# First loads over three queues, a first layer by single units, and filler products on TensorE, in a DeltaNet block followed by a gated feed-forward block

## The chip, the cores and the metric

The kernel runs on one core of a Trainium2 chip. The metric is the device time of one execution in microseconds; three runs of a kernel give a median. A profile of one more execution gives the span of that core, which is shorter than the device time of the same run. Engines are PE (TensorE; PEld is its weight load), DVE (VectorE), ACT (ScalarE), POOL (GpSimd) and SP (SyncE, which here only issues transfers).

## The reference

For each of 4 x 8 heads, a state of 48 x 48 is carried through 768 tokens, and the result goes through a feed-forward block:

```python
for t in range(S):
    y[:, :, t] = einsum('bhd,bhde->bhe', q[:, :, t], state)
    v_old = einsum('bhde,bhd->bhe', state, kt)          # kt = k / (|k| + 1e-6)
    state = state + bt * einsum('bhd,bhe->bhde', kt, vt - v_old)
x = y.transpose(0, 2, 1, 3).reshape(3072, 384)
h = x @ w_in                                            # 384 x 2048
out = (h * cos(h)) @ w_out                              # 2048 x 384
```

q, k, v and beta are float32; both weights are float64 in memory, so they arrive as pairs of 32-bit words and are narrowed on the chip.

## The kernel before

The tokens are cut into 24 units of 32 tokens (all heads, all batches); two units make a pair. For each unit, k and q are loaded (`load`, L323; four transfers each), transposed on PE (`turn`, L489), and multiplied with each other (`gram`, L507). The scaled product (`gram_keys`, L518) is written to DRAM (`gram_put`, L538) and read back in another layout (`gram_get`, L547; two transfers per pair). There a triangular inverse is built column by column for a whole pair (`invert`, L576 and L583): for pair 0 on DVE in PSUM, for all the others on POOL. It is written to DRAM (`put`, L592) and read back per unit (`get`, L601; four transfers).

Then comes the serial part: `through_state` (L618) multiplies the unit's keys and queries with the state, `right_side` (L633) subtracts, `solve` (L645) applies the inverse, `solve_out` (L653) scales, `update` (L666) and `update_out` (L674) change the state, `within` (L683) adds the part inside the unit. `features` (L700) transposes the result into `x_ffn`. Unit 0 has no product with the state.

A pair's 256 tokens then pass the feed-forward block: eight steps of `hidden` (L719; six matmuls of 128x128 by 128x256 each, filling one of two PSUM banks `p_h`), each followed by ACT `turns` (L732), DVE `rest` (L736), ACT `cos` (L743, L744) and DVE `gate` (L751), and then the second layer. Pair 0 uses the plain second layer (`output`, L761); later pairs use seven products of Strassen's scheme (`product`, L805, sums on DVE). The weights come in 28 pieces (12 of w_in, 16 of w_out): SP load (L396), ACT split (L404, L406), DVE shift (L410, L415), POOL add (L419). A step of the first layer of pair 0 needs the first 3, 6, 9 or 12 of the w_in adds.

No engine chooses at run time. A planner (`Order`) plays the tasks through when the kernel is built, each with a cost, a due time and the buffers it takes, and writes one order per engine, which the engine then follows strictly. What a task may start with is decided by buffers: `kq`, `one`, `two` and `p_h` in PSUM, nine large SBUF buffers `g` shared by weight pieces, gates and squares. The planner also models the arrival of PE's instructions in blocks of 256 (`stall`), counting the matmuls written so far. Inside the kernel's opening, loads of units 0 and 1, the constants and beta are issued outside the planner, in program order.

```python
load(0, "k")                       # SP
...
load(0, "q", nc.scalar)            # ACT
...
load(1, "q")                       # SP
load(1, "k", nc.gpsimd)            # POOL, behind two transfers of consts and four of beta
```

Of the kernel before, what the change touches and what calls it, by code (L numbers as in the profile page):

```python
# [11 lines left out]
FP = mybir.dt.float32  # L12
I32 = mybir.dt.int32
# [4 lines left out]
C = 32  # L18
DP = 64
SPLIT = 2  # L20
# [26 lines left out]
class Order:  # L47
# [8 lines left out]

    WINDOW = 133.06
    LAG = {"PE": 0.2, "DVE": 0.15, "ACT": 0.15, "POOL": 0.2, "SP": 2.0}
    IN_FLIGHT = 8
    STICK = 4.14  # L60
    CHANGE = 0.15
# [8 lines left out]

    def __init__(self, bufs, free):
        self.bufs, self.free = bufs, free
        self.tasks, self.users, self.tiles = {}, {}, {}
        self.written, self.there = 0, {}

    def add(
# [7 lines left out]
        for tag, t in makes:  # L84
            self.tiles[t] = tag

    def stall(self, key, now, commit):

        n = int(1.007 * self.COUNT[key[0]] + 0.5)
        if key[0] == "state" and key[1] == 0:  # L90
            n = 0
        cost, stall, there = self.tasks[key][1], 0.0, {}
        for i in range(self.written + 1, self.written + n + 1):
            t = now + cost * (i - self.written) / n + stall
            if (i + self.PHASE + self.AHEAD) % self.BLOCK == 0:
                there[(i + self.PHASE + self.AHEAD) // self.BLOCK + 1] = t + self.FETCH
            if (i + self.PHASE) % self.BLOCK == 0:
                block = (i + self.PHASE) // self.BLOCK
                stall += max(0.0, there.get(block, self.there.get(block, 0.0)) - t)
        if commit:  # L100
            self.written += n
            self.there.update(there)
        return stall

    def run(self, wrote):
# [28 lines left out]
        while events:  # L134
# [28 lines left out]
            for engine, heap in ready.items():  # L163
# [3 lines left out]
                item = min(able, default=None)  # L167
                if item is None:
                    continue
                if engine == "PE":  # L170
# [49 lines left out]
def kernel(  # L220
# [58 lines left out]
    def bank(tag, shape, name):  # L279
        bufs = {"kq": 1, "two": 1, "one": 1, "h": 2}[tag]  # L280
        return psum.tile(shape, FP, name=name, tag=tag, bufs=bufs)
# [7 lines left out]
    def quarter(b):  # L289
        return slice(C * b, C * b + C)  # L290
# [43 lines left out]
    near = 130 + C  # L334
    for cols in (slice(0, near), slice(near, consts_np.shape[1])):
        nc.gpsimd.dma_start(out=consts[:, cols], in_=consts_dr.ap()[:, cols])
    ident = consts[:, 0:128]
# [6 lines left out]
    for b in range(B):  # L344
        nc.gpsimd.dma_start(
            out=bq[C * b : C * b + H].rearrange("p n t -> p (n t)"), in_=beta[b]
        )
    load(1, "q")
    load(1, "k", nc.gpsimd)

# [183 lines left out]
    def gram_put(n):  # L534
        m = n // 2
        if m not in gbs:
            gbs[m] = dram.tile([2, H, B, C, C], FP, name="g_dr")
        nc.sync.dma_start(  # L538
            out=gbs[m][n % 2].rearrange("h b j i -> (b j) h i"), in_=gs.pop(n)
        )  # L540

    def gram_get(m):

        g_dr = gbs[m]
        gbs[m] = work.tile([128, C, C], FP, name="gb", bufs=GBS)
        for a in range(SPLIT):
            nc.sync.dma_start(  # L547
                out=gbs[m][half(a)].rearrange("p j i -> p (j i)"),
                in_=g_dr.rearrange("u h b j i -> (u h b) (j i)"),
            )  # L550
# [44 lines left out]

    def get(n):

        zts[n] = work.tile([128, H, C], FP, name="zt")
        z_dr = z_drs[n // 2].rearrange("r s u h b i -> u b (r s) h i")[n % 2]
        for b in range(B):  # L600
            nc.sync.dma_start(out=zts[n][quarter(b)], in_=z_dr[b])  # L601

# [110 lines left out]
    gates, p_hs, turns, rests, p_os, outs = ({} for _ in range(6))  # L713

    def hidden(p, f):
        p_h = p_hs[p, f] = bank("h", [128, 2, TOK], "p_h")
        for i in range(2):
            for t in range(KT):
                nc.tensor.matmul(  # L719
                    p_h[:, i],  # L720
                    w_in[:, t, (f + i) * 128 : (f + i + 1) * 128],
                    xts[p][:, t],
                    start=(t == 0),
                    stop=(t == KT - 1),
                )
# [4 lines left out]
    def hidden_turns(p, f):  # L730
        turns[p, f] = ffn_pool.tile([128, 2, TOK], I32, name="turns")
        nc.scalar.activation(turns[p, f], p_hs[p, f], AF.Copy, scale=TURN)  # L732

    def hidden_rest(p, f):
        r = rests[p, f] = ffn_pool.tile([128, 2, TOK], FP, name="r")
        nc.vector.scalar_tensor_tensor(  # L736
            out=r, in0=p_hs[p, f], scalar=TURN, in1=turns.pop((p, f)),
            op0=ALU.mult, op1=ALU.subtract,
        )
# [6 lines left out]
    def hidden_gate(p, f):  # L746
        if f % 4 == 0:
            gates[p, f // 4] = ffn_pool.tile(
                [128, 4, TOK], FP, name="g_ffn", tag="g", bufs=GATES
            )  # L750
        nc.vector.tensor_tensor(  # L751
            out=gates[p, f // 4][:, f % 4 : f % 4 + 2],
            in0=rests.pop((p, f)),
            in1=p_hs.pop((p, f)),
            op=ALU.mult,
        )
# [105 lines left out]
    def store(p, i):  # L862
# [4 lines left out]
        )  # L867


    order = Order(  # L870
# [4 lines left out]
        ),  # L875
        free={"SP": 5.5, "ACT": 5.6, "POOL": 6.2, "DVE": 6.0, "PE": 6.0},
    )
    add = order.add
    VECTOR = {0: "one"}
    W_IN, W_OUT, LOADS = 62.2, 48.42, -16.83  # L880
    PLAIN = range(1)
    outs_done = [None]
    START = 64.59
    FIRST, STEP = 4.18, 5.64
    BASE = [START + (8 * FIRST + (p - 1) * 8 * STEP if p else 0) for p in range(NU // 2 + 2)]

    def inverse(m):
        add(("gram_get", m), "SP", 1.2, lambda: gram_get(m),
            [("gram_put", 2 * m), ("gram_put", 2 * m + 1)], makes=[("gb", ("gb", m))],
            uses=[("g_dr", m)], moves=2.2)  # L890
        held = VECTOR.get(m)
        z = ("p_i", m) if held else ("z", m)
        add(("eye", m), "ACT", 0.65, lambda: invert_eye(m, held),
            [("gram_put", 2 * m + 1)] + ([("eye", m - 1)] if m else []),
            makes=[(held or "z", z)])
        deps = [("eye", m), ("gram_get", m)]
        ends = [0, 4, 8, 12, 16, 20, 24, C - 1]
        for i, (x, y) in enumerate(zip(ends, ends[1:])):
            each = (0.2, 0.001) if held else (0.323, 0.00178)
            cost = sum(  # L900
                2 * (each[0] + each[1] * (j // SPLIT + 1) * (C - 1 - j)) for j in range(x, y)
            )
            add(("inv", m, i), "DVE" if held else "POOL", cost,
                lambda x=x, y=y: invert(m, held, range(x, y)), deps,
                uses=[("gb", m)] if y == C - 1 else [])
            deps = [("inv", m, i)]
        if held:
            add(("inv_out", m), "ACT", 0.65, lambda: invert_out(m), deps,
                makes=[("z", ("z", m))], uses=[z])
            deps = [("inv_out", m)]  # L910
        add(("put", m), "SP", 0.45, lambda: put(m), deps, makes=[("z_dr", ("z_dr", m))],
            uses=[("z", m)], moves=2.6)

    def unit(n):
        m, second = n // 2, n % 2
        for x, prev in (("k", 2 * len(kps)), ("q", 2 * len(qps)), ("v", 4)):
            if n < 2 and x != "v":
                add((x, n), "SP", 0.0, lambda: None)
                continue
# [50 lines left out]
        if second:  # L970
            inverse(m)
        add(("get", n), "SP", 1.9, lambda: get(n), [("put", m)], makes=[("zt", ("zt", n))],
            uses=[("z_dr", m)], moves=1.4)

# [5 lines left out]
            uses=[("vp", m)] if n else [])  # L980
        add(("solve", n), "PE", 0.75, lambda: solve(n), [("right", n), ("get", n)],
            makes=[("one", ("p_u", n))], uses=[("zt", n), ("rhs", n) if n else ("vp", m)])
# [18 lines left out]
    def gated(p):  # L1001
        for f in range(0, FT, 2):
            deps = [("features_out", 2 * p + 1)]
            if p == 0:
                deps += [("add", t) for t in range(KT * (f // 4 + 1))]
            if p or f:
# [10 lines left out]
            add(("gate", *key), "DVE", 0.73, lambda f=f: hidden_gate(p, f),  # L1017
                [("cos", *key)] + ([("gate", p, f - 2)] if f % 4 else []),
                makes=[] if f % 4 else [("g", ("gates", p, f // 4))],
                uses=[("h", *key), ("r", *key)], due=BASE[p] + f // 2 * STEP + 8)  # L1020
# [11 lines left out]
    def plain(p):  # L1032
        last = outs_done[0]
        for i in range(2):
            for k in range(FT // 4):
                deps = [("gate", p, 4 * k), ("gate", p, 4 * k + 2)]
                if p == 0:
                    deps += [("add", 12 + t) for t in range(4 * k + 4)]
                if last:
# [74 lines left out]

    add(("beta",), "DVE", 1.3, spread_beta)
    for n in range(NU):
# [69 lines left out]
```

## Time and profile before

| | |
|---|---|
| device time, median of 3 runs | 712.05 us (711.9 to 712.48) |
| the profiled run | 709.21 us, span 707.4 us, mean granted clock 0.955 |
| PE busy | 642.0 us, 91% of the span |
| DVE, ACT, POOL busy | 400.3, 281.5, 344.1 us |
| chain that ended last | PE 85%, DMA 4%, POOL 3%, DVE 3%, issue 2% |
| first matmul of the first layer (L719) | 79.15 us |

The profile cuts the span into 40 slices of 17.7 us and gives the busy share of each engine in tenths. PEclk is the granted clock of PE in tenths of the full one. In the chain, "issue" is time in which an engine waited for nothing that the profile shows. An arrow with an engine or a transfer names what ended an idle time.

### The profile page before, as it was taken

Reading aid. Unit: us, or ns where it says so; the run is one execution under the profiler, and the core shown is the slowest. Engines: PE = TensorE matmul, PEld = TensorE weight load, DVE = VectorE, ACT = ScalarE, POOL = GpSimd, SP = SyncE. Lnnn points to the kernel's source line nnn. Section 1 sums busy time; section 2 is a strip of 40 time slices with the busy share of each in tenths; the row PEclk is TensorE's granted clock in tenths of the full one; section 3 lists DMA queues with packets and bytes.
Section 4 is the critical chain, followed back from the end, with each engine's and each line's share of the span. In section 5 each row is a group of like instructions: output and inputs, shape, how many; then the busy total and the mean of one; then the engine's idle time right before and its main releaser. Section 6 shows DMA issues by size and latency. Waiting matters only on the chain.

```text
span 707.4 us, 25090 instructions
## 1 busy us (share of the span) xinstructions
PE 642.0 (91%) x11000; PEld 564.3 (80%) x11000; DVE 400.3 (57%) x804; ACT 281.5 (40%) x482; POOL 344.1 (49%) x738
## 2 busy tenths in 40 slices
PE   3206989999999999999999999999999999999985
PEld 2205767768988988988988988988989989988975
DVE  4995568967655645546546546545635535544441
ACT  4423467742443532532533533533433433432420
POOL 6468957868608508518518518518318328200000
PEclk9555899999999999999999999999999999999999
DMA  9888663562223233133223133231221220100000
GB/s 176 211 161 197 122 193 80 135 125 58 36 56 71 39 64 67 32 74 66 45 60 66 29 77 64 38 74 37 38 51 37 37 52 14 31 23 4 1 23 22
DMA packets 162700, 49.25 MB, mean 70 GB/s; under 512 B 154208, under 2 KB 157296, under 8 KB 162592
## 3 DMA queue, kind: packets, MB, share of 16 engines
q1 hardware_dynamic: 161120, 46.82, 32.1%
q8 instruction: 86, 1.41, 0.9%
q0 software_dynamic: 384, 0.64, 0.4%
q10 hardware_dynamic: 1088, 0.20, 0.2%
q14 instruction: 22, 0.18, 0.1%
HBM read 36.62 MB, written 11.01 MB: 67 GB/s over the span
## 4 chain that ended last, share of the span: by engine, by line
PE 85%; DMA 4%; POOL 3%; DVE 3%; issue 2%; ACT 1%; SPq 1%; ACTq 0%; DVEq 0%; POOLq 0%
PE p_h L719 35%; PE p_out L805 30%; PE p_kq L618 4%; PE p_kq L683 3%; PE p_s L666 3%; PE p_out L761 3%; PE p_u L645 3%; PE p_t L489 2%; PE p_g L507 2%; DMA pairs<-in_moe_w_in_dram 2%; POOL part L576 1%; POOL z L583 1%; DMA qp<-in_q_dram 1%; DMA gb<-g_dr 1%; DMA kp<-in_k_dram 1%
## 5 line engine op out<-in xcount | busy, mean ns | idle before, releaser
L719 PE MATMUL p_h<-x_ffn,w_in 128*128 128x256 f32 x1152 | 264.9, 383 | 2.4 <-DVE g_ffn L751 1.6
L719 PEld LDWEIGHTS p_h<-x_ffn,w_in 128*128 128x128 f32 x1152 | 216.9, 191 | 32.0 <-DVE g_ffn L751 1.5
L576 POOL TENSOR_TENSOR part<-z,gb 128x126 f32<-128x126 f32 (+22 forms) x341 | 136.1, 399 | 210.7 <-DMA gb<-g_dr 185.3
L583 POOL TENSOR_TENSOR z<-z,part 128x126 f32<-128x126 f32 (+22 forms) x341 | 134.3, 394 | 26.7
L805 PE MATMUL p_out<-w_out,g_ffn 128*128 128x192 f32 x704 | 133.6, 334 | 2.8 <-DVE o L853 1.6
L736 DVE SCALAR_TENSOR_TENSOR r<-p_h,turns 128x512 f32<-128x512 f32 x96 | 66.1, 689 | 113.8 <-ACT turns L732 113.7
L732 ACT ACTIVATE turns<-p_h 128x512 int32<-128x512 f32 x96 | 56.9, 592 | 169.1 <-PE p_h L719 169.0
L805 PEld LDWEIGHTS p_out<-w_out,g_ffn 128*128 128x128 f32 x704 | 113.6, 190 | 9.5 <-ACT o L842 3.3
L805 PE MATMUL p_out<-w_sum,g_ffn 128*128 128x192 f32 x528 | 96.3, 329 | 1.8 <-DVE o L853 1.8
L751 DVE TENSOR_TENSOR g_ffn<-r,p_h 128x512 f32<-128x512 f32 x96 | 65.6, 683 | 48.0 <-ACT r L744 48.0
L805 PEld LDWEIGHTS p_out<-w_sum,g_ffn 128*128 128x128 f32 x528 | 86.3, 190 | 4.9 <-DVE o L853 3.1
L821 DVE TENSOR_TENSOR g_ffn<-g_ffn 128x256 f32<-128x256 f32 x176 | 80.5, 480 | 10.8 <-PE p_out L805 8.9
L743 ACT ACTIVATE r<-r 128x512 f32<-128x512 f32 x96 | 60.7, 632 | 58.2 <-DVE r L736 58.1
L744 ACT ACTIVATE r<-r,halfpi 128x512 f32<-128x512 f32 x96 | 69.3, 722 | 3.1
L853 DVE SCALAR_TENSOR_TENSOR o<-p_out,o 128x192 f32<-128x192 f32 x77 | 26.5, 356 | 59.7 <-PE p_out L805 59.2
L489 PE MATMUL p_t<-consts,kp 128*128 128x128 f32 x96 | 16.9, 306 | 41.9 <-DMA vp<-in_v_dram 29.5
L489 PEld LDWEIGHTS p_t<-consts,kp 128*128 128x128 f32 x96 | 12.9, 157 | 44.6 <-issue 38.5
L694 ACT COPY y<-p_kq 128x384 f32<-128x384 f32 x24 | 11.5, 478 | 76.7 <-PE p_kq L683 76.7
L448 POOL TENSOR_TENSOR knrm<-ksum,halves 128x16 f32<-128x16 f32 (+1 forms) x14 | 36.4, 2602 | 9.8 <-DVE ksum L436 7.6
L618 PEld LDWEIGHTS p_kq<-st,kq_t 48*32 48x32 f32 x2944 | 29.5, 106 | 9.6 <-issue 8.8
L618 PE MATMUL p_kq<-st,kq_t 48*32 48x48 f32 x2944 | 33.1, 215 | 3.9 <-issue 3.2
L653 DVE TENSOR_TENSOR u<-p_u,bz 128x768 f32<-128x768 f32 x24 | 23.0, 956 | 17.1 <-PE p_u L645 17.1
(65 smaller groups left out, 547.0 us busy)
## 6 DMA issues: line engine op xcount, KB each, us to landing
pairs<-in_moe_w_in_dram SPq DMA_DIRECT2D x12, 512.0 KB
gb<-g_dr SPq DMA_DIRECT2D x24, 256.0 KB
pairs<-in_moe_w_out_dram SPq DMA_DIRECT2D x16, 384.0 KB
vp<-in_v_dram SPq DMA_DIRECT2D x96, 48.0 KB
out_dram<-o SPq DMA_DIRECT2D x24, 192.0 KB
kp<-in_k_dram SPq DMA_DIRECT2D x92, 48.0 KB
qp<-in_q_dram SPq DMA_DIRECT2D x92, 48.0 KB
g_dr<-g SPq DMA_DIRECT2D x24, 128.0 KB
```

What stands on the lines that cost most here:

```text
L489: nc.tensor.transpose(p_t[:, a, j], src[:, 2 * j : 2 * j + 2], ident)
L576: eng.tensor_tensor(out=part, in0=z[:, 0:rows, j, None].to_broadcast(shape), in1=a[:, j, None, j + 1 :].to_broadcast(shape), op=ALU.mult,)
L583: eng.tensor_tensor(out=behind, in0=behind, in1=part, op=ALU.subtract)
L618: nc.tensor.matmul(p_kq[quarter(b), par, a, j], kq_t[rows48(par), a, j, quarter(b)], st[rows48(par), b // 2, j, b % 2], start=(j == 0 and ...
L719: nc.tensor.matmul(p_h[:, i], w_in[:, t, (f + i) * 128 : (f + i + 1) * 128], xts[p][:, t], start=(t == 0), stop=(t == KT - 1),)
L732: nc.scalar.activation(turns[p, f], p_hs[p, f], AF.Copy, scale=TURN)
L736: nc.vector.scalar_tensor_tensor(out=r, in0=p_hs[p, f], scalar=TURN, in1=turns.pop((p, f)), op0=ALU.mult, op1=ALU.subtract,)
L743: nc.scalar.activation(r, r, AF.Abs)
L744: nc.scalar.activation(r, r, AF.Sin, bias=halfpi, scale=-2.0 * math.pi)
L751: nc.vector.tensor_tensor(out=gates[p, f // 4][:, f % 4 : f % 4 + 2], in0=rests.pop((p, f)), in1=p_hs.pop((p, f)), op=ALU.mult,)
L805: nc.tensor.matmul(p_o, left(p, e // 2, a)[:, e % 2], right(e, b), start=(e == 0), stop=(e == FT // 2 - 1), skip_group_check=True,)
L821: nc.vector.tensor_tensor(out=left(p, k, to), in0=left(p, k, one), in1=left(p, k, two), op=op)
```

## The change

Three things are done, and the planner's constants are set anew, so that the order changes on all engines.

1. Loads. k of unit 1 moves from POOL to SP, ahead of q of unit 1; the far part of the constants moves on POOL behind beta. Pair 0's second `gram_get` transfer, and two of the four `get` transfers of units 0 and 1, move from SP to ACT's queue.
2. First layer of pair 0 by single units (`hidden_one`): a step takes four column tiles for one unit's 128 tokens, twelve matmuls of 128x128 by 128x128, in place of two column tiles for 256 tokens. Steps 0 to 3 need unit 0 alone, and the gates of all four groups are opened by them.
3. Filler (`warm_up`): where the planner sees PE idle between 44 and 80 us of its own clock, it writes a product of the identity with constants, 128x128 by 128x256, into the PSUM bank of the second layer, which nobody reads. 37 of them are written: 21 after the gram of units 2 and 3; 4 after the turn of unit 4; 4 and 2 around the update of unit 0; 3 and 3 around that of unit 1.

```diff
-    WINDOW = 133.06
+    WINDOW = 74.02
+    WARM = 44.0, 80.0
-    STICK = 4.14
+    STICK = 4.01
@@ stall
-        n = int(1.007 * self.COUNT[key[0]] + 0.5)
+        n = int(n * 1.034 if self.written < 1000 else n * 1.0054 + self.rest)
@@ run
                 if item is None:
+                    if engine == "PE" and self.WARM[0] <= now < self.WARM[1]:
+                        self.warm()
+                        self.written += 4
+                        free[engine] = now + 0.45
...
@@ opening
-    for cols in (slice(0, near), slice(near, consts_np.shape[1])):
-        nc.gpsimd.dma_start(out=consts[:, cols], in_=consts_dr.ap()[:, cols])
+    nc.gpsimd.dma_start(out=consts[:, :near], in_=consts_dr.ap()[:, :near])
...
+    nc.gpsimd.dma_start(out=consts[:, near:], in_=consts_dr.ap()[:, near:])
+    load(1, "k")
     load(1, "q")
-    load(1, "k", nc.gpsimd)
@@
+    def hidden_one(f):
+        unit, k = f // 8, f // 2 % 4
+        p_h = p_hs[0, f] = bank("h", [128, 4, 128], "p_h")
+        for i in range(4):
+            for t in range(KT):
+                nc.tensor.matmul(p_h[:, i],
+                    w_in[:, t, (4 * k + i) * 128 : (4 * k + i + 1) * 128],
+                    xts[0][:, t, unit * 128 : (unit + 1) * 128],
+                    start=(t == 0), stop=(t == KT - 1))
+    def warm_up():
+        nc.tensor.matmul(flat_out[:, 0:256], ident, consts[:, 0:256], start=True, stop=True)
@@
-    W_IN, W_OUT, LOADS = 62.2, 48.42, -16.83
+    W_IN, W_OUT, LOADS = 57.87, 67.5, 4.07
-    START = 64.59
-    FIRST, STEP = 4.18, 5.64
+    START = 40.69
+    FIRST, STEP = 3.12, 5.86
@@ inverse, pair 0
+            add(("gram_get", m), "SP", ..., lambda: gram_get(m, range(1)), puts, ...)
+            add(("gram_get2", m), "ACT", ..., lambda: gram_get(m, range(1, 2), nc.scalar), puts, ...)
@@ unit, n < 2
+            add(("get", n), "SP", ..., lambda: get(n, range(2)), [("put", m)], ...)
+            add(("get2", n), "ACT", ..., lambda: get(n, range(2, 4), nc.scalar), [("put", m)], ...)
@@ gated, p == 0
+                deps = [("features_out", f // 8)]
+                deps += [("add", t) for t in range(KT * (f // 2 % 4 + 1))]
@@ plain, p == 0
+                    deps = [("gate", p, 8 * i + 2 * k)]
```

In the new order, POOL computes the norms of pair 2 (L448) behind the inverse of pair 1 rather than inside it, and then all eight open w_in adds in a row. SP issues the last three w_in pieces one after another, ahead of k of unit 6.

## The prediction

> **What bounds the kernel now.** I read the page first, its slices before its sums. PE is busy 91% of the span, but the first slices are not, and the granted clock is low exactly there:
>
> ```profile
> PE   3206989999999999999999999999999999999985
> PEclk9555899999999999999999999999999999999999
> DMA  9888663562223233133223133231221220100000
> ```
>
> From the sixth slice on PE is the bound: in the stretches of 10 us from 160 to 680 it stands at 9.3 to 10.0. Nothing in that stage is removed or added, so only the first 110 us can change the time. Next, the stretches of that stage (columns: length, then busy us and instructions of PE, PEld, DVE, ACT, POOL, granted clock, DMA share, GB/s):
>
> ```profile
> 50.00:60.00 10.00, 3.95 (x72) 3.32 (x72) 6.26 (x10) 3.39 (x6) 8.76 (x16) 0.50 0.73 162
> 60.00:70.00 10.00, 8.02 (x355) 7.01 (x355) 5.45 (x13) 3.99 (x8) 9.00 (x15) 0.50 0.93 205
> 70.00:80.00 10.00, 8.09 (x258) 6.94 (x241) 6.31 (x10) 4.19 (x8) 8.58 (x14) 0.63 0.68 119
> 80.00:90.00 10.00, 9.67 (x165) 8.01 (x164) 4.85 (x10) 6.08 (x12) 9.25 (x7) 1.00 0.67 152
> 90.00:100.00 10.00, 8.12 (x239) 6.73 (x238) 8.72 (x18) 8.39 (x17) 5.33 (x12) 1.00 0.90 271
> 100.00:110.00 10.00, 8.90 (x126) 7.14 (x130) 4.41 (x8) 3.01 (x7) 4.91 (x10) 0.83 0.15 41
> ```
>
> Units 0 and 1 are solved at half clock, transfers run at 0.7 to 0.9 of their time, POOL is full. Third, PE in order of time (start, length, instruction):
>
> ```profile
> 53.45 1.09 PE L489 MATMUL p_t<-consts,kp 128*128 128x128 f32 x4 [29.49 <-DMA vp<-in_v_dram]
> 57.04 2.01 PE L645 MATMUL p_u<-vp,zt 32*32 32x48 f32 x64 [1.65 <-issue]
> 79.15 5.45 PE L719 MATMUL p_h<-x_ffn,w_in 128*128 128x256 f32 x24
> 88.48 0.88 PE L645 MATMUL p_u<-rhs,zt 32*32 32x48 f32 x64
> 101.10 0.30 PE L618 MATMUL p_kq<-st,kq_t 48*32 48x48 f32 x10 [2.99 <-issue]
> 101.33 4.53 PE L719 MATMUL p_h<-x_ffn,w_in 128*128 128x256 f32 x12
> ```
>
> A solve costs 2.01 us at 57 and 0.88 at 88. A stall of 2.99 us without a named cause splits the state product of unit 3; after it a first-layer step takes 4.53 us in place of 2.8, as the clock has dropped. (The wait at 53.45 carries a false name: vp isn't read there. The turn of unit 4 needs the bank that DVE's `tt` of unit 3 leaves at 53.35.) Last, POOL and SP:
>
> ```profile
> 38.86 0.24 POOL L576 TENSOR_TENSOR part<-z,gb 128x31 f32<-128x31 f32 x1 [10.39 <-DMA gb<-g_dr]
> 64.67 2.90 POOL L448 TENSOR_TENSOR knrm<-ksum,halves 128x16 f32<-128x16 f32 x1
> 73.61 2.53 POOL L419 TENSOR_TENSOR w_in<-w_in,pairs 128x512 uint32<-128x512 uint32 x2
> 73.96 0.40 SPq L592 DMA_DIRECT2D z_dr<-z  x1
> 78.69 5.86 SPq L601 DMA_DIRECT2D zt<-z_dr  x8
> ```
>
> POOL's inverse of pair 1 runs from 38.86 to 73.66. Behind it stand eight w_in adds (1.26 us each) and, over two transfers, the solve of unit 2 at 88.48. So the ramp has two chains: PE's own (53 to 79) and POOL's.
>
> **What the Trainium skill says.** "TensorE: Matmul & The Clock Gate", Part 1 (What's actually happening): after an idle window of some 3.4 us the clock is half, after a busy one full. The trace agrees: 0.50 through the pauses up to 76, full after PE ran without a pause from 72.71 on; about 4 us. Same page, LDWEIGHTS: a load costs columns / 1.2 ns, an estimate of 107 ns for 128 columns, so a 128-wide pass can still hide it. Turns, which load for every 128-wide pass, start 0.44 us per four (116.63 to 117.07), 110 ns each: agreed. "DMA: Bandwidth & Descriptors", Issuing engines are not separate DMA queues: a second issuing engine saves only issue time. Here an issue takes about 0.45 us (L323: 1.79 for four) against 4 to 6 us to landing.
>
> **The change part by part.** *Loads.* k of unit 1 lands at 12.07 today, 5.04 us after its last issue. SP's queue would have it earlier, perhaps by 2 us. But SP then issues four more transfers (1.8 us) before the `gram_put`s it reaches at 16.75, and the bytes ahead are the same at some 200 GB/s. The ACT half of `gram_get` stands behind ACT's split of the third weight piece (20.52 to 21.7 today), and the eye copy, the fourth split and DVE's fourth shift, which precedes the inverse, queue behind ACT's wait. I let DVE's inverse start at 27.6 as now (bounds −1.5, +1.5) and POOL's at 38.9 (same bounds). The ACT half of `get` saves two issues, 0.9 us, of the 57.04; ACT's next split waits behind it, with slack.
>
> *Filler.* Nothing holds the 21: they run right behind the gram that ends at 24, over by 42 even at half clock (0.86 us each; at full clock 0.43, as L719's 2.59 us for six of this size), and PE idles again until 53.4. They cost and give nothing. The turn (2.0 us) and four fillers (3.45 at half clock) make 5.5 us without a pause up to 58.9, more than the 4 us seen; so full clock before 59. The solve of unit 0 waits for them: 58.0 instead of 56.5, but takes 0.88, ending at 58.9 against 59.05. Then, at full-clock durations from this trace: fillers 1.73 (DVE's u, 0.96, hides inside), update 0.89, within 0.88, fillers 0.86, features 0.5, state 1.3: 65.2. New step 0 of the first layer 2.6: 67.8. Solve 0.88, fillers 1.3, update, within 1.77, fillers 1.3, features 0.5, state 1.3, gram 0.86: 75.8. Today's PE starts its first step at 79.15 and does that gram only at 84.53.
>
> *POOL.* Norms out of the inverse: it ends at 70.7 (73.66 − 2.9); norms then, adds 4 and 5 by 76.2: step 1 can't start sooner. That step and the turn of unit 5 end at 79.8. For unit 2, `put` at 70.8, then eight k and q transfers (3.6 us), `get` 75 to 77, landing after 2.4 to 4 us: 79.5 to 81. I take the solve of unit 2 at 81.5 (bounds 79 and 85).
>
> *Comparing there.* Today's PE has, at its 88.48, one first-layer step (2.6) and one gram (0.86) more behind it. Lead: 88.48 − 81.5 − 3.46 = **3.5 us** (bounds 0 and 6).
>
> *Stalls.* Today's loses 2.99 + (4.46 − 2.79) = 4.66 us at 98 to 106. Counting two weight loads and two passes per matmul (one each for a transpose), this stall and the smaller one at 71.97 (0.74) lie 1,274 apart, five blocks of 256 less a few; the new counts fit both to within two. So the planner now knows the places. But its wait of 3.5 us for a block is short: the block asked for 38 instructions before the last boundary came after some 7.5 us in both stalls, with transfers dense. In the new order four boundaries after 81 (second step there, state of unit 3, solve of unit 3, state of unit 4) leave 3 to 4.6 us. I keep 1.5 us of loss: **−3.2** (bounds −4.7 and +3). Two before 81 (state products of units 1 and 2) are in the 4 us that separate PE's 75.8 from 79.8 and in the bound of 85.
>
> *N = 128.* 8 steps x 24 passes x 3 ns: **+0.6** (bound: 0 and +3, if loads show). Gates write 512 elements as before: 0. ACT and DVE work per step is unchanged.
>
> Sum: −3.5 − 3.2 + 0.6 = −6.1 against the span of 707.4. That run took 709.21 while the three others have a median of 712.05; I take the same difference off: **706.0 us**.
>
> **The rivals.** A, everything early: transfers land 1.5 us sooner, no stall: lead 6, stall −4.7, the pause of 1.28 at 136.5 gone too: −12, 700. For it: exact block counts. Against: DMA at 0.9.
> B, the clean start is eaten: fillers mostly run too early, the solve of unit 2 comes at 84, stalls like today's at the new places: −1.0 + 0.6 and up to 1 either way: 711.5, no change. For it: the 7.5 us.
> C, slower: the fillers are paid at half clock. One place: PE between 55 and 77. If the clock isn't released before the first layer's step 0 (4.3 us, part slow), then solve, fillers, update, within, fillers, features, state take 2.0 + 3.45 + 3.06 + 1.7 + 0.9 + 1.8 = 12.9 from 58.9: step 0 ends at 76, and the 7.9 us of full-clock work, step 1 and turn bring the solve of unit 2 to 88: lead −3; with N = 128 and stalls as today 715.5. It decides as soon as that solve starts later than 85. Against it: 4 us without pause sufficed twice, at 12 to 17 and 72 to 76.
> D, the change doesn't do what it says: the clock stays as today and no step of unit 0 comes early, only the norms' shift acts: 2.9 us earlier for POOL less some handing over, −2, 710.
>
> **How the numbers follow.** Main case 45%, 706; A 20%; B 18%; C 12%; D 5%. The range from 698.5 to 713 holds main, A, D and most of B and leaves C out. A measurement tells some 0.2% (1.4 us) from no change. Faster: main, A, D and a third of B: 0.76. Same: the rest of B: 0.12. Slower: C: 0.12.
>
> **What would show it.** Granted clock 1.0 from about 58 and solve of unit 0 at 0.9 us; 21 fillers over long before 53; first layer from 65; POOL's inverse of pair 1 ended near 70.7; solve of unit 2 near 81.5; "issue" waits of PE after 81 under 2 us. Wrong if the inverse of pair 0 starts more than 2 us off 27.6, if fillers run at half clock at 60, or if a step of twelve takes over 2.8 us.

## The result, and the profile after

The changed kernel is slower: 720.84 us (719.69 to 723.42) against 711.97 us (711.5 to 712.48), four runs each; ratio 1.0129, interval 1.0098 to 1.0161. The profiled run took 719.78 us with a span of 717.8 us, 10.4 us over the span of before (8.9 us by the medians).

The slices of the page, in the same three rows as before:

```profile
PE   4807889989999999999999999999999999999995
PEclk9967799999999999999999999999999999999999
DMA  7886474364214134134135035043122120100000
```

From the tenth slice on PE is as full as before. The clock row is less low (6 and 7 tenths in place of 5), but low up to the same 90 us. The stretches of 10 us (columns as before):

```profile
50.00:60.00 10.00, 4.04 (x14) 3.62 (x15) 6.81 (x11) 1.92 (x4) 8.83 (x16) 0.50 0.72 170
60.00:70.00 10.00, 7.68 (x249) 5.93 (x248) 4.24 (x6) 5.34 (x11) 8.43 (x21) 0.99 0.76 223
70.00:80.00 10.00, 9.09 (x172) 8.25 (x175) 3.29 (x6) 1.35 (x4) 9.53 (x13) 0.66 0.47 79
80.00:90.00 10.00, 7.76 (x302) 6.98 (x292) 8.21 (x14) 3.03 (x6) 6.55 (x5) 0.88 0.25 59
100.00:110.00 10.00, 7.72 (x139) 7.12 (x138) 7.52 (x15) 5.69 (x13) 6.00 (x9) 0.90 1.00 205
```

The clock is full at 60, as intended, and gone again at 70. PE in order of time (start, length, idle before it and what ended that) shows why:

```profile
55.96 1.09 PE L504 MATMUL p_t<-consts,kp 128*128 128x128 f32 x4 [21.52 <-DMA vp<-in_v_dram]
57.69 3.17 PE L914 MATMUL p_out<-consts 128*128 128x256 f32 x8
60.79 0.88 PE L664 MATMUL p_u<-vp,zt 32*32 32x48 f32 x64
70.91 0.96 PE L637 MATMUL p_kq<-st,kq_t 48*32 48x48 f32 x58 [2.27 <-issue]
71.80 5.49 PE L740 MATMUL p_h<-x_ffn,w_in 128*128 128x128 f32 x24
86.60 0.23 PE L637 MATMUL p_kq<-st,kq_t 48*32 48x48 f32 x1 [2.24 <-issue]
87.40 4.57 PE L740 MATMUL p_h<-x_ffn,w_in 128*128 128x128 f32 x24
92.77 0.88 PE L664 MATMUL p_u<-rhs,zt 32*32 32x48 f32 x64
107.66 0.37 PE L702 MATMUL p_kq<-u,tt 32*32 32x48 f32 x14 [2.23 <-issue]
107.95 4.57 PE L740 MATMUL p_h<-x_ffn,w_in 128*128 128x128 f32 x24
129.71 0.31 PE L637 MATMUL p_kq<-st,kq_t 48*32 48x48 f32 x14 [1.50 <-issue]
156.46 5.71 PE L757 MATMUL p_h<-x_ffn,w_in 128*128 128x256 f32 x19 [2.89 <-DVE g_ffn L794]
```

Four waits without a named cause cut small products in two, each at one of the counted block ends (every 256 instructions), and three of them are followed by a step of the first layer at 4.57 to 5.49 us in place of 2.9. The solve of unit 2 starts at 92.77, later than before (88.48). The last line is something new: PE stands 2.89 us for a gate of the second pair. How much was lost ahead of it, the first step of pair 1 tells, where both kernels have done the same products, the fillers apart. Before, and changed:

```profile
118.91 2.86 PE L719 MATMUL p_h<-x_ffn,w_in 128*128 128x256 f32 x12
```

```profile
129.96 5.45 PE L757 MATMUL p_h<-x_ffn,w_in 128*128 128x256 f32 x24
```

The changed kernel is 11.05 us behind there, 14.9 us at 311.20 (326.11), and 10.66 us where the last products of the second layer begin (674.96 and 685.62): a loss as large as the final one is made in the first 130 us. POOL and SP, on the other hand, kept to the forecast within some 2 us: the inverse of pair 1 runs from 41.00 to 72.0, and

```profile
72.11 0.39 SPq L610 DMA_DIRECT2D z_dr<-z  x1
77.34 1.88 SPq L620 DMA_DIRECT2D zt<-z_dr  x4
```

so `zt` of unit 2 was issued 13 us ahead of the solve that needs it. PE's own chain set the time, not POOL's.

### The profile page after: what moved, and what is told of

The parts are those of the page before. It is cut to its first block, busy times and chain, and to the rows that moved or that the text cites. A ratio compares the mean times of both kernels' runs of the same rounds, so it can differ in the third digit from the quotient of the medians.

```text
span 717.8 us, 25428 instructions
## 1 busy us (share of the span) xinstructions
PE 659.3 (92%) x11170; PEld 584.2 (81%) x11170; DVE 400.7 (56%) x804; ACT 281.2 (39%) x482; POOL 340.6 (47%) x734
## 4 chain that ended last, share of the span: by engine, by line
PE 87%; DMA 4%; DVE 4%; issue 2%; SPq 1%; ACT 1%; POOL 0%; ACTq 0%; DVEq 0%
PE p_h L757 32%; PE p_out L848 29%; PE p_kq L637 4%; PE p_h L740 4%; PE p_kq L702 3%; PE p_u L664 3%; PE p_s L685 3%; PE p_out L804 3%; PE p_t L504 2%; PE p_g L522 2%; PE p_out L914 1%; DVE p_i L601 1%; DVE part_v L594 1%; PE p_z L719 1%; SPq L338 1%
## 5 line engine op out<-in xcount | busy, mean ns | idle before, releaser
L757 PE MATMUL p_h<-x_ffn,w_in 128*128 128x256 f32 x1056 | 243.9, 383 | 4.7 <-DVE g_ffn L794 2.9
L594 POOL TENSOR_TENSOR part<-z,gb 128x126 f32<-128x126 f32 (+22 forms) x341 | 131.6, 386 | 219.6 <-DMA gb<-g_dr 194.0
L757 PEld LDWEIGHTS p_h<-x_ffn,w_in 128*128 128x128 f32 x1056 | 198.0, 191 | 31.9 <-issue 5.5
L601 POOL TENSOR_TENSOR z<-z,part 128x126 f32<-128x126 f32 (+22 forms) x341 | 137.7, 404 | 26.7
L848 PE MATMUL p_out<-w_out,g_ffn 128*128 128x192 f32 x704 | 130.6, 332 | 2.4 <-DVE o L896 1.6
L848 PE MATMUL p_out<-w_sum,g_ffn 128*128 128x192 f32 x528 | 93.9, 327 | 1.6 <-DVE o L896 1.6
L740 PE MATMUL p_h<-x_ffn,w_in 128*128 128x128 f32 x192 | 29.3, 321 | 0.6 <-issue 0.6
```

The lines of the kernel that those rows point to most:

```text
L594: eng.tensor_tensor(out=part, in0=z[:, 0:rows, j, None].to_broadcast(shape), in1=a[:, j, None, j + 1 :].to_broadcast(shape), op=ALU.mult,)
L601: eng.tensor_tensor(out=behind, in0=behind, in1=part, op=ALU.subtract)
L740: nc.tensor.matmul(p_h[:, i], w_in[:, t, (4 * k + i) * 128 : (4 * k + i + 1) * 128], xts[0][:, t, unit * 128 : (unit + 1) * 128], start=(t ...
L757: nc.tensor.matmul(p_h[:, i], w_in[:, t, (f + i) * 128 : (f + i + 1) * 128], xts[p][:, t], start=(t == 0), stop=(t == KT - 1),)
L848: nc.tensor.matmul(p_o, left(p, e // 2, a)[:, e % 2], right(e, b), start=(e == 0), stop=(e == FT // 2 - 1), skip_group_check=True,)
```

## The experiments

All ratios are to the kernel before, whose median was 710.1 to 712.1 us. "Anew" means that the planner made its orders again.

**Each part on the kernel before.** First the loads alone (x4), an edit that leaves the order of all computation:

```diff
+    nc.gpsimd.dma_start(out=consts[:, near:], in_=consts_dr.ap()[:, near:])
+    load(1, "k")
     load(1, "q")
-    load(1, "k", nc.gpsimd)
...
+            (nc.scalar if m == 0 and a else nc.sync).dma_start(
...
+            (nc.scalar if n < 2 and b > 1 else nc.sync).dma_start(out=zts[n]
```

> The kernel before with the first loads dealt out as in the change, alone: k of unit 1 on SP, far consts behind beta, half of the first inverse's input and of its first two results on ACT. PE's order is that of before. Theory L: the inverse of pair 0 starts 2 to 2.5 us later than 27.6 and the time rises by 1.5 to 3 us. Theories S and F: within 1 us of before.

Measured 0.9987 (0.9972 to 1.0002). The inverse of pair 0 starts at 29.59, 2 us later than before, but the first step of the first layer at 78.33 (before 79.15): the delay is absorbed. The other way round, the changed kernel with its loads as before (x2):

> The changed kernel with all first loads as before: k of unit 1 on POOL behind consts and beta, second half of the inverse's input and of its result on SP. Order of everything else the same. Theory L: the inverse of pair 0 starts at 27.6 to 28 instead of 30.1, that of pair 1 at 39 instead of 41.0, and the time falls by 2 to 3 us. Theories S and F: the ramp starts earlier but PE stalls at the same instructions (14th record of the within of unit 0, 70th of the state of unit 1 and so on), and the time falls by under 1.5 us.

Measured 1.0079 (1.0052 to 1.0105), but the span is 716.6, 1.2 us under the changed kernel's; the waits sit at the same instructions (2.57, 2.35 and 2.70 us), and DVE's inverse still starts at 30.16. By the medians up to 0.5% could be the loads' (the intervals touch), by the spans 1.2 us; on the kernel before they cost nothing. They are not the main cause. Then the counts alone (x7), and the planner's numbers alone (x10):

```diff
-        n = int(1.007 * self.COUNT[key[0]] + 0.5)
+        n = int(n * 1.034 if self.written < 1000 else n * 1.0054 + self.rest)
```

> The kernel before with the changed kernel's count of instructions alone in the planner (1.034 up to 1000, 1.0054 and the rest carried on after), the plan made anew; loads, layer, constants as before. The prediction's step (the better counts put small products clear of the block ends and save 3.2 us after the solve of unit 2): 703 to 706 of span, ratio 0.990 to 0.997, no wait of 2 to 3 us in the state product of unit 3. Theory (the counts move the waits, since a block takes 4 to 9 us to come in the first 130 us and any order runs into some end): ratio 0.998 to 1.004, with a sum of waits for instructions before 130 us that is within 2 us of that of before.

Measured 1.0011 (0.9997 to 1.0026). A wait of 3.11 us at 102.80 stands where before had 2.99 at 101.10: knowing the counts did not take it away.

```diff
-    WINDOW = 133.06
+    WINDOW = 74.02
...
-    W_IN, W_OUT, LOADS = 62.2, 48.42, -16.83
+    W_IN, W_OUT, LOADS = 57.87, 67.5, 4.07
-    START = 64.59
+    START = 40.69
```

> The kernel before with the changed kernel's numbers of the planner alone (window, STICK, due times), its loads, pairs of units and counts as before, the plan made anew. Theory N (the numbers cost by themselves): slower, ratio 1.003 to 1.012, with a wait of PE of 2 us or more for a gate of the second pair near 150. Theory S (the numbers do nothing but set other places for block ends): 0.997 to 1.005 and no such wait.

Measured 1.0091 (1.0071 to 1.0111). PE waits 5.55 us for gates up to 200 us. But the reverse, the changed kernel with the old numbers (x9),

> The changed kernel with the planner's numbers (window, STICK, due times of w_in, w_out and of the first layer) as before; loads, single units, counts and fillers as changed, the plan made anew. Theory N (the new numbers make w_out's pieces due later than the second pair's gates need DVE for, so PE waits 2.9 to 4.6 us for a gate of the second pair near 150, and the order of the first 100 us is worse): ratio 0.997 to 1.008, no wait of over 1.5 us for a gate between 130 and 170. Theory S (only the place of the block ends and the fillers' time count): ratio 1.008 to 1.02 again, waits for instructions of 6 us or more in sum before 130 us.

came to 1.0142 (1.0088 to 1.0196), with a wait of 2.71 us for instructions at 126.20 and 3.32 us for gates. Its start is better: four steps, all at full clock and with no wait for a gate, are done at the solve of unit 2 (92.45), where the changed kernel has done two (92.77). At the same products it is 9.1 us ahead of the changed kernel at 194 us, and 2.6 us at the end: most of it is lost again in the steady part. The numbers are no cause that could be undone by itself: each set has its own plan, and a plan is good or bad with all the rest.

**Fillers and block ends.** The changed kernel with its plan kept and `warm_up` emitting nothing (x1):

```diff
-        nc.tensor.matmul(flat_out[:, 0:256], ident, consts[:, 0:256], start=True, stop=True)
+        pass
```

> The changed kernel without the 37 fillers, all else in the same order on every engine. Theory S (instruction supply: PE runs through blocks of 256 instructions in 1.3 to 5 us where their arrival took 3.5 to 9 us from the end of the block before, and each stall also halves the clock): the block ends move by up to 148 instructions to other places, the clock stays at half through the solves of units 0 and 1, so fewer stalls there (under 2 us together before the solve of unit 2, against 5.5), and the time falls by 1 to 4 us. Theory F (the fillers themselves hold the chain up: they run 1 to 3 us past what they hide): time falls by 4 to 8 us, solve of unit 2 at 87 or earlier. Theory L (the dealt-out loads start the inverse of pair 0 late): no change, within 1 us, and the inverse of pair 0 still starts near 30.1.

Measured 1.0170 (1.0123 to 1.0217), slower still. The solve of unit 2 comes at 88.45, 4.3 us earlier, and the first step of pair 1 8 us earlier (121.86 against 129.96), only 2.95 us behind the kernel before at the same products. All of that gain is lost later: without the 37 fillers the block ends lie 148 instructions elsewhere, and between 200 and 700 us PE waits 8.0 us for instructions (changed kernel: 1.9; waits over 0.3 us summed). The three largest waits come at 258.45, 418.93 and 579.0, every 160 us: the plan repeats, so one bad place is paid again and again. Against the kernel before this version is 1.1 us behind at 142 us and 15.8 us where the last second-layer products begin, each time at the same products. Now the 21 early fillers alone left out (x3),

```diff
+        warms[0] += 1
+        if warms[0] > 21:
+            nc.tensor.matmul(flat_out[:, 0:256], ident, consts[:, 0:256], start=True, stop=True)
```

> The changed kernel without the 21 fillers that run at 24 to 34 us, long before the solve; the other 16 stay. Nothing waits for those 21, so by theories F and L nothing changes (within 1 us). Theory S: the block ends move by 84 instructions, so the stalls leave their places: none inside the within of unit 0 at its 14th record; instead at or behind its end (42 records later), in the state of unit 1 near record 112 instead of 70, and the stall of 2.2 us in the within of unit 2 moves to the state of unit 3 (near its 4th record). Total within 3 us either way.

which lie in an idle place that ends 20 us after them: 1.0250 (1.0199 to 1.0302). The waits of the solve moved by 84 instructions, the number that was left out, and 8.0 us of waits came up between 200 and 700 us. And all 37 early, none in the solve (x5; all places from the solve of unit 2 on as in the changed kernel):

> The changed kernel with all 37 filler products in the idle place behind the gram of unit 3 and none in the solve; the number of instructions ahead of the solve of unit 2, and so every later place of a block end, is as in the changed kernel. Theory (the later sixteen fillers cost their 9.4 us in a serial chain, and what the kernel without fillers then lost was the moved block ends): the solve of unit 2 starts at 88 to 89.5 as without fillers, the waits after it stay where the changed kernel has them (about 2.2 us in the within product of unit 2, 1.5 in the state product of unit 4) and the steady part shows no waits of 2 us for instructions; span 710 to 714, ratio to before 0.998 to 1.008. Rival (the fillers keep the clock up and pay for themselves): more steps at half clock between 60 and 100, ratio 1.012 or more. Rival (the solve's start doesn't matter, a later wait takes the gain): solve of unit 2 at 88.5 but span 716 to 719.

Measured 1.0147 (1.0092 to 1.0201). The theory falls: the sixteen later fillers (9.4 us of PE) are gone from the solve, and its unit 2 still starts at 92.83:

```profile
69.43 1.11 PE L637 MATMUL p_kq<-st,kq_t 48*32 48x48 f32 x70 [0.69 <-issue]
81.17 1.76 PE L637 MATMUL p_kq<-st,kq_t 48*32 48x48 f32 x126 [1.18 <-DVE st L693]
85.97 0.28 PE L637 MATMUL p_kq<-st,kq_t 48*32 48x48 f32 x1 [3.04 <-issue]
87.12 4.91 PE L740 MATMUL p_h<-x_ffn,w_in 128*128 128x128 f32 x24
```

PE comes to the same block end earlier and waits longer there: it goes on at 85.97, the changed kernel at 86.60. Products at half clock and waits for DVE took the rest. This version and the one without fillers differ only by 37 fillers in an idle place, done 15 us before PE's next product: the 148 instructions of shift alone move the first step of pair 1 from 121.86 to 129.96. Last, the kernel before with 57 fillers in its idle place, which move its block ends by 228 (x8):

```diff
+                if key == ("gram", 3):
+                    self.warm()
...
+        for _ in range(57):
+            nc.tensor.matmul(flat_out[:, 0:256], ident, consts[:, 0:256], start=True, stop=True)
```

> The kernel before, its order untouched, with 57 filler products in the idle place behind the gram of unit 3: they move the later instructions by 228 against the block ends, so that the ends lie 28 instructions further on in the order. Theory (waits are set by the place of the block ends alone): the solve of unit 2 within 1 us of 88.5, the waits of 2.99 and 1.67 us in the state product of unit 3 and behind it gone or moved by 28 instructions, others of the steady part moved too; span 702 to 710, ratio 0.994 to 1.004. Rival (idle-time products cost or give nothing, the waits belong to the data): waits of 2.99 and 1.67 at the same instructions, ratio 0.998 to 1.002. Rival (fillers warm the clock): first solve shorter by 1 us or more and the lead kept to the end.

Measured 0.9989 (0.9963 to 1.0016). The wait of 2.99 us moved by those 28 instructions, to 106.52 (1.88 us), and in place of one of 0.74 us at 72.71 stand two of 0.97 and 1.27 us at 67.90 and 72.76: the waits follow the places, and their sum from 60 to 200 us is no smaller, 4.1 us against 3.7.

**w_out's pieces.** One number back, anew (x12):

```diff
-    W_IN, W_OUT, LOADS = 57.87, 67.5, 4.07
+    W_IN, W_OUT, LOADS = 57.87, 48.42, 4.07
```

> The changed kernel with one number back, the due time of w_out's pieces (48.42 in place of 67.5), the plan made anew. Theory N in its narrow form (w_out's pieces come too late, and DVE does them together with the second pair's gates at 142 to 157): the wait of 2.89 us for a gate at 156 gone, ratio 1.003 to 1.010. If w_out isn't it: the wait stays within 1 us, ratio 1.010 or more. If the pieces of w_in are pushed back by it, the first step of the first layer comes after 73 and the solve of unit 2 after 94.

Measured 1.0084 (1.0055 to 1.0113). The wait at 156.46 is gone, the longest for a gate of the second pair is 1.20 us, and the solve of unit 4 still comes at 165.83; the waits for instructions stay (2.27, 2.12 and 3.18 us). The solve of unit 2 stands at 92.83 as in the changed kernel, but with one first-layer step and one gram more behind it, some 3.7 us of work. This is a part of the loss, not the loss.

**Pairs again, with and without fillers.** The first layer by pairs, loads, fillers, numbers and counts as changed, anew (x6):

```diff
-        if p == 0:
-            return hidden_one(f)
...
```

> The changed kernel with the first pair's first layer by pairs of units again (tiles of 256 columns), loads, fillers, counts and the planner's constants as changed; the plan is made anew. Theory (single units cost nothing in themselves, the fillers and the waits for instructions do): still 1.004 to 1.016 over before, the first hidden step of the first pair not before 84, fillers of 9 us or more still in the chain, steps at half clock still there. Rival (the single units are the loss: twice the instructions and twice the weight loads): within 0.3% of before, the solve of unit 2 at 87 to 89.

Measured 1.0206 (1.0157 to 1.0255): the slowest version but one. Without fillers in it and in the planner's count (x11):

```diff
-                        self.written += 4
...
-        nc.tensor.matmul(flat_out[:, 0:256], ident, consts[:, 0:256], start=True, stop=True)
+        pass
```

> The kernel before with the new loads, counts and numbers of the planner, but without single units and without fillers, the plan made anew. If the fillers made the version by pairs the slowest of all (1.0206): ratio back at 0.998 to 1.006, the solve of unit 2 at 87 to 89. If the numbers did (theory N): ratio 1.010 to 1.02 still, with the wait for a gate near 150.

Measured 1.0006 (0.9986 to 1.0026). PE's order up to 126 us is the same in both but for the fillers and one swap of neighbours, and up to the solve of unit 2 the version *with* fillers is ahead (90.73 against 92.56). Then SP's orders part. Without fillers, the four pieces of w_out in one go:

```profile
128.18 4.64 SPq L410 DMA_DIRECT2D pairs<-in_moe_w_out_dram  x4
149.66 5.57 PE L754 MATMUL p_h<-x_ffn,w_in 128*128 128x256 f32 x24 [1.00 <-DVE g_ffn L788]
```

With fillers, three of the four stand behind q and v on SP's queue, POOL waits 5.10 us, DVE's shifts pile up in front of a gate, and PE waits 4.65 us for it:

```profile
135.28 2.91 SPq L411 DMA_DIRECT2D pairs<-in_moe_w_out_dram  x3
136.82 1.02 POOL L434 TENSOR_TENSOR w_out<-w_out,pairs 128x384 uint32<-128x384 uint32 x1 [5.10 <-DMA vp<-in_v_dram]
154.03 7.55 PE L755 MATMUL p_h<-x_ffn,w_in 128*128 128x256 f32 x24 [4.65 <-DVE g_ffn L789]
```

A further 6.8 us of waits for instructions fall between 200 and 700 us there, against 0.9 without fillers. So fillers might cost by themselves, or only through the plan and the places. A square of four tells it: pairs or single units, with no fillers or with 64 that the planner doesn't count. 64 fillers are 256 instructions, one whole block, so the later block ends stay where they are, and all orders are kept (18 is 26 for the single units, which have fewer idle places).

```diff
+        warms[0] += 1
+        for _ in range(18 if warms[0] == 1 else 1):
+            nc.tensor.matmul(flat_out[:, 0:256], ident, consts[:, 0:256], start=True, stop=True)
```

> The version by pairs without fillers (x11), every order of every engine kept, plus 64 fillers that the planner doesn't count: 46 in the idle place behind the gram of unit 3, 18 in the places of the solve where the plan has PE idle. 64 fillers are 256 instructions, so every later block end stays where it was. Theory P (fillers themselves save 1 to 2 us, by the clock, and what cost 2 per cent in x6 was the plan that they moved: w_out's pieces behind k, q and v on SP's queue): the solve of unit 2 at 90.5 to 92, no wait of over 1.5 us for a gate near 150, ratio 0.995 to 1.001. Rival F (fillers cost in themselves, wherever): ratio 1.008 or more, the wait near 150 back.

> The changed kernel without fillers and without their count in the plan, made anew: the new loads, counts, numbers, and single units in the first layer. Beside x11 it differs in the single units alone. If single units cost by themselves (twice the instructions for the same columns, so more block ends in the dense part): 1.004 to 1.012 over before. If they are neutral: 0.998 to 1.004, as x11. A wait for a gate near 150 of over 2 us would say that the plan, not the units, is what is seen.

> x14 with 64 fillers that the planner doesn't count (46 early, 18 in the solve), all orders and all later block ends as in x14. Theory P: against x14 by 0 to 2 us faster, the solve of unit 2 earlier by 0 to 2 us, since the first steps run at full clock. Rival F: slower than x14 by 3 us or more. If x15 falls within 0.3% of before, then what made the changed kernel slower is the plan with fillers counted, and neither the fillers nor the units as such.

| | no fillers | 64 fillers |
|---|---|---|
| pairs | 1.0006 (0.9986 to 1.0026), x11 | 0.9996 (0.9976 to 1.0016), x13 |
| single units | 1.0084 (1.0053 to 1.0115), x14 | 1.0088 (1.0054 to 1.0123), x15 |

Fillers, all else kept, are worth nothing and cost nothing, within the 0.2 to 0.35% of these intervals. In x13 the gate that waited 4.65 us in x6 waits 1.10 at most, as theory P had it; its gain of 1 to 2 us isn't seen. The 46 early ones move the block ends inside the solve, and a wait of 2.96 us at 70.37 took what the clock gave: the solve of unit 2 starts at 92.48, in x11 at 92.56. The plans with single units are 0.8% slower. What becomes of the early layer, the stretch from 80 to 100 us shows, in x11, x13, x14 and x15 in turn:

```profile
80.00:100.00 20.00, 20.00 (x386) 16.02 (x387) 13.97 (x27) 11.96 (x22) 12.24 (x10) 1.00 0.61 148
```

```profile
80.00:100.00 20.00, 20.00 (x396) 16.02 (x395) 17.92 (x31) 12.38 (x23) 12.73 (x10) 1.00 0.59 145
```

```profile
80.00:100.00 20.00, 15.33 (x322) 14.36 (x323) 15.95 (x28) 11.14 (x20) 11.98 (x9) 1.00 0.62 144
```

```profile
80.00:100.00 20.00, 15.87 (x363) 14.84 (x352) 15.85 (x28) 11.34 (x21) 12.48 (x10) 1.00 0.64 147
```

By pairs PE is busy for all of the 20 us, by single units it stands for 4.67 and 4.13 us. In x15 the idle places are these, with DVE's part of it:

```profile
83.10 1.94 PE L739 MATMUL p_h<-x_ffn,w_in 128*128 128x128 f32 x16 [1.19 <-issue]
85.90 0.63 PE L503 MATMUL p_t<-consts,kp 128*128 128x128 f32 x4 [0.86 <-DVE tt L541]
96.24 2.92 PE L739 MATMUL p_h<-x_ffn,w_in 128*128 128x128 f32 x24 [1.69 <-DVE g_ffn L793]
83.04 1.44 DVE L429 TENSOR_SCALAR w_out<-w_out 128x384 uint32<-128x384 uint32 x1
84.41 0.68 DVE L793 TENSOR_TENSOR g_ffn<-r,p_h 128x512 f32<-128x512 f32 x1
90.47 0.42 DVE L532 TENSOR_TENSOR g<-p_g,bs 128x256 f32<-128x256 f32 x1 [2.92 <-PE p_g L521]
95.41 0.69 DVE L793 TENSOR_TENSOR g_ffn<-r,p_h 128x512 f32<-128x512 f32 x1 [0.38 <-ACT r L781]
```

The layer starts at 69 in place of 81, but a step needs one of two banks, and a bank comes free with a gate on DVE. DVE has norms and w_out's shifts in front of the gates, and stands 2.92 us for a gram that PE does after a step. At the first step of pair 1, with the same products behind them, x14 is at 125.75 and x15 at 124.42, x11 at 125.09 and x13 at 125.12: 12 us of earlier start have come to nothing. In x14 that double step takes 7.02 us and in x15 8.20, at half clock behind waits for instructions (1.19 and 1.59 us in x14, 0.64 and 2.00 us in x15), against 5.45 by pairs. But this is not the 0.8%. A later place with the same products done is the transpose behind the state product of unit 5, again in x11, x13, x14 and x15:

```profile
173.13 0.49 PE L718 MATMUL p_z<-consts,y 128*128 128x128 f32 x3
```

```profile
174.07 0.49 PE L718 MATMUL p_z<-consts,y 128*128 128x128 f32 x3
```

```profile
174.53 0.55 PE L718 MATMUL p_z<-consts,y 128*128 128x128 f32 x3
```

```profile
174.39 0.55 PE L718 MATMUL p_z<-consts,y 128*128 128x128 f32 x3
```

Single units are 1.4 us behind there without fillers and 0.3 us with them, while the spans differ by 5.7 and 3.5 us. Most of the 0.8% arises after the first pair, where both versions work by pairs of units, in orders that differ. So it is a cost of the plan that comes with single units; a cost of the units themselves is not shown.

No version tried is measurably faster than before; 0.9987 and 0.9989 both have 1 inside the interval.

## Why the prediction was wrong

The forecast of 706.0 (698.5 to 713) missed by 14.8 us, and on the wrong side. By its own sum, and by the spans: lead at the solve of unit 2, foretold +3.5, measured 88.48 - 92.77 - 3.46 = -7.75. After that, foretold a gain of 3.2 less 0.6 for N = 128, measured a loss of 10.4 - 7.75 = 2.65. The difference, 11.25 + 5.25 = 16.5, is the whole from -6.1 to +10.4.

- *The step that failed*: "I take the solve of unit 2 at 81.5", with the two block ends before it put "in the 4 us that separate PE's 75.8 from 79.8". PE's own chain came through the gram at 87.40 instead of 75.8. Of these 11.6 us, 2.6 are the late turn of unit 4 (55.96 against 53.4), 5.46 are three waits for instructions (0.95, 2.27 and 2.24), and 2.9 the first step of the layer, 5.49 in place of 2.6, at the clock that the second wait had dropped; together 10.9. Step 1 ran at 4.57 in place of 2.6 for the same reason. I had priced those ends as slack that could be spent once; they are serial in PE's chain, and each cost its wait and the clock behind it. Even with the fillers' time taken out (x5) the chain came no earlier, and with the waits laid otherwise the early layer was held up by gates (x14, x15). The lead that the sum rests on was in no version with single units: by the same sum they stand at the solve of unit 2 from 1.4 us (x9, x14) to 8.0 us (x2) behind the kernel before.
- *Comparing there.* That "only the first 110 us can change the time" was wrong as a rule, and the place of comparison did not decide. The version by pairs without fillers (x11) is 4.9 us behind at the solve of unit 2 and ends level (1.0006); the changed kernel without fillers (x1) is 3.4 us behind there and ends 15.6 us of span behind. No product was added to the steady part, but the new order and the moved block ends changed its waits.
- *Loads.* Inverse of pair 0 at 30.09, outside 27.6 +/- 1.5. The transfers that SP has to issue before the `gram_put` were counted (1.8 us), and it slipped from 16.75 to 18.88. I then let the start stand all the same. On the kernel before such a delay is absorbed (x4). In the changed kernel it is the late turn of unit 4, 2.6 of the 11.6 us; x2 couldn't take it away, since there DVE's inverse stood behind the norms and started at 30.16 too.
- *Filler.* The 21 ran from 24.14 to 34.43, as foretold; the clock was full when the solve of unit 0 began at 60.79 with 0.88 us, as foretold (58.0), though the four fillers ahead of it still took 3.17 us, mostly at half clock. Full clock was granted at 60.27, 4.3 us after the turn began. The reading of before was short, too: full clock came at 77.46 there, 4.75 us after 72.71 and not 4. "They cost and give nothing" holds for their time (x13, x15), not for the 84 instructions by which they move the block ends: without them 1.0250 in place of 1.0129.
- *POOL.* Inverse ended at 72.0 (70.7 foretold), `get` issued at 77.34 (75 to 77). The mechanism was right and was no longer the bound.
- *Stalls.* The places were right: all waits lie at the counted ends. Foretold was that the planner, knowing them, would keep most of the 4.66 us. x7 shows that counts alone gain nothing: from a restart at one end to the restart at the next PE took 3.68 (x11) to 9.23 us (changed kernel) where it stood, the plan reckons with 3.5, and 256 instructions of small products run in 1.4 to 1.8 us at full clock. The orders tried shift such waits; none of the traces is without one before 130 us.
- *N = 128.* Right: full-clock steps of twelve took 2.84 to 2.94 (before 2.75 to 2.86 for six of 256 columns). The sign of being wrong, "over 2.8 us", was passed by these lengths, but was set too low: five of the six such steps before, up to 119 us, pass it as well.
- *Rival C* had the side and its deciding point (a solve of unit 2 later than 85), with another mechanism: the fillers were paid mostly at full clock (9.4 us for sixteen), and taking them away brought nothing (x5). What no rival named is the place of the block ends as the cause, the cost of the new orders beyond the first pair, and that of a late w_out.

What stays open: the single units can't be had without a plan of their own, so the 0.8% is theirs together with the orders that follow from them, and why those orders lose most of it after 174 us was not traced. Between x15 (1.0088) and the changed kernel (1.0129) lies what counting the fillers does to the plan; the intervals overlap, and only for pairs (0.9996 against 1.0206) is it shown. That PE waits there for a block of its instructions agrees with the Trainium skill ("Runtime: NRT & Kernel Launch", Instruction fetch mechanics: each engine's sequencer fetches its program by DMA in blocks of 256 instructions, 16 KiB, while it executes the one before) and with the places, which moved by the number of instructions put in or taken out (x3, x8). The transfers settle it: in all 17 traces PE's waits of 0.3 us or more without a named cause, 105 of them from 60 us on, end 1.20 to 1.68 us after the end of a 16 KB transfer of the kind "instruction" on queue q8. Earlier ones, at the turn of unit 4 and at the first product of unit 0's solve (57.04 before, 59.64 in x8), have no such transfer within 17 us and are of another kind. The same section calls a crossing mostly hidden; here, in the dense parts, a crossing that shows costs 0.3 to 3.3 us. Why one fetch takes longer than another was not tried: no fetch was stretched or shortened by itself.

## What to carry to other kernels

A start that comes earlier is worth what the next thing in the same engine's order lets through: follow the earlier work to the first place where both versions have done the same products, compare there, and compare again further on, since an order that repeats pays for a bad place each time. Waits inside a serial chain are added, not set against slack, and each is priced with the clock behind it. Instructions put into idle time move all later block ends; if they are to be tested for what they do, add a whole block of them and keep the orders.

## What was not expected of the hardware

- A wait of some 2 us is enough for half clock: 2.27, 2.24 and 2.23 us were followed by steps of 5.49, 4.57 and 4.57 us in place of 2.9. The Trainium skill ("TensorE: Matmul & The Clock Gate", Part 1) puts the idle window at some 3.4 us. The traces show the length but not the rule: within a trace all changes of the granted clock lie on a grid of 3.41 us (half from 70.51 for 6.83 us, from 87.57 for 3.41 and from 108.05 for 3.41 in the changed kernel). In the 17 traces, between 60 and 690 us, a stretch of this grid at full clock with PE idle for 1.79 us or more was always followed by half clock, one with 1.36 us or less never, and between 1.4 and 1.8 us both occur. So half of a stretch is about enough, and what counts is the idle time inside one: x8's wait of 1.88 us lay across two, 1.06 and 0.82, and cost no clock.
- The granted clock can read 1.00 while PE runs at half: without fillers (x1) the row shows 1.00 from 0 to 80 us, where the trace has no record of the clock up to 74.28, and there an update takes 1.56 us and a within product 1.50, against 0.89 and 0.88 later. Durations tell it, the row doesn't. The same part of the page warns that such records have been unreliable, and these runs agree.
- The transfers of 16 KB of the kind "instruction" that end PE's waits start 2.2 to 3.3 us and end 1.2 to 1.7 us ahead of the restart (x5: 83.60 to 84.54, restart at 85.97; changed kernel: 83.98 to 85.11, restart at 86.60). That they are PE's own, the count tells: 87 of them on q8 in the changed kernel and 86 before, against 2 x 11,170 and 2 x 11,000 instructions of PE and PEld in the trace, 87.3 and 85.9 times 256.
